# An adaLN block with an S4 convolution and a Mish MLP: the convolution regrouped with 512 channels in the free dimension, constant weights, and corner turns through DRAM

## The chip, the cores and the metric

The program runs on one core of one Trainium2 chip. The metric is the device time of one execution in microseconds (us), as the median of several runs. One execution was also taken with the hardware profiler; all rows of a trace come from that one. Engines are named as in the profile: PE is TensorE's matmul, PEld its weight load, DVE is VectorE, ACT is ScalarE, POOL is GpSimd, and SP is the engine that issues most of the DMA transfers.

## What is computed

The input x has 2048 rows (tokens) of 512 channels, in float32. A vector c gives six vectors of 512 by `silu(c) @ w_mod`: shift, scale and gate for the two halves of the block.

```
sa, ca, ga, sb, cb, gb = split(silu(c) @ w_mod, 6)
h = layernorm(x) * (1 + ca) + sa
x = x + ga * s4(h)              # convolution along the 2048 tokens
h = layernorm(x) * (1 + cb) + sb
x = x + gb * (mish(h @ w1 + b1) @ w2)       # 512 -> 1792 -> 512

s4(u): for each channel d: dt = exp(log_dt), A, B, C of 128 complex states n
  K[d, l] = Re sum_n C[n] * exp(dt A[n] l) * (discretised B)[n],  l = 0 .. 2047
  y[:, d] = causal convolution of u[:, d] with K[d, :], plus u * Dskip
```

The convolution is done as a transform along the tokens, a complex product for each channel, and the inverse transform, with two steps of matmuls each way.

## The kernel before

One function, `s4_block`, holds the whole program; a scheduler orders the instructions of each engine by the priorities that the code sets. It has three stretches.

**The start (0 to about 42 us).** Loads of the parameters (`raw`, L173), of x (`xr`, L195, four transfers of 1 MB) and of weights; the states' parameters are worked out on VectorE (`params`).

**The convolution (to 418 us).** The 512 channels are worked in 32 groups `k` of 16 channels. A slot of the loop holds, for different groups at once:

- Kernel generation. `s_ang` (L344) makes the angles of the powers of exp(dt A) in PSUM as `pang`, two matmuls of 256 columns for each half; `s_ri` (L355, L357) rounds them to whole turns on VectorE, for some groups with ScalarE's help (L349, adding a magic constant), and `s_neg` (L362) subtracts the rounded turns by a matmul with `negid`. `s_sin` (L145, L367) makes sines and cosines into the tile `ec`. `s_mag` multiplies coarse exponentials `co` into the two magnitudes m1 and m2 (L377, L380), and `s_comb` (L387 to L391) multiplies them into `ec`. `s_kgen` (L402) contracts `ec` over the states into `pkg`, ScalarE copies that to `ks` (L407), and `s_ka` (L418) makes the first step of the kernel's transform, `pka`, copied to the tile `gk` (L426).
- The transforms of the input. `s_ua` (L526), a transpose `put` (L536), and the second step with the constant `mf` as the moving or the stationary operand (L546, `pub` and `pkb`). Here the data or `gk` and the constant meet in matmuls of 128 columns, with channels on the partitions.
- The complex product on VectorE (L583 to L585, tile `q`), a transpose `pt` (L590) to `yt`, the first inverse step `pib` (L601), the copy `z` (L603), a transpose `pt` (L611) to `zt`, and the last inverse step `pia` (L637), which is added to x on VectorE (L639). The sum goes to the DRAM tensor `x2d` in another row order.

```
def s_ri(k):
    ri = gen.tile([P, 2, 512], F16, tag="ri", name=f"ri{k}", bufs=1)
    RI[k] = ri
    if RID[k]:
        V.tensor_scalar(ri, PA[k], MAGIC, MAGIC, op0=OP.add, op1=OP.subtract)
...
def s_neg(k):
    for e in range(2):
        T.matmul(PA[k][:, e, :], negid, RI[k][:, e, :], start=False, stop=True, skip_group_check=True)
```

**The MLP (437.86 us to the end).** `ln_load` reads rows from x2d (L774), VectorE takes the statistics and normalises (L781, L790), TensorE transposes (`pln`, L799), and `hf`, `hh` are the modulated rows and their high and low parts. w1 and w2 are kept as high and low parts too (`w1h`, `w1l`, `w2h`, `w2l`), so each product is three matmuls (`pm`, L897, and `po`, L915; 1344 matmuls in all). Mish runs on ScalarE (`mh`), `mah` and `mal` are its two parts, and `ot` is the output, stored by SP (`out`).

Of the kernel before, what the change touches and what calls it, by code (L numbers as in the profile page):

```python
# [28 lines left out]
NCO = 28  # L29
NPRE = 8  # L30
SL = {"p2": 0, "p3": 2, "ls0": 5, "raw": 2, "p0": 5, "ls1": 8, "co0": 6, "vis": 6, "h0": -5, "h1": -2}
HA = 4
NUG = 2
MS = [[3, 0], [5, 2], [0, 4], [1, 6], [2, 8], [4, 9]]
BN = [0, 0, 0, 1]
NS = 1
HS0 = [2, 3, 3, 2]
SPA = 0
RID = [1, 0, 0, 0, 1, 0, 0, 0, 1, 0, 0, 0, 1, 0, 0, 1, 1, 0, 0, 0, 1, 1, 0, 1, 1, 0, 1, 0, 1, 1, 0, 1]
PRI = {"mm": 0.933, "ug": 0.775, "tm": 0.608, "inva": 0.817, "sin": 1.075, "ml": 0.533, "st": 0.933, "par": 0.625, "ri": -0.108, "kgen": 0.05, "p": -0.475, "sr": 1.575, "t2": 0.15, "ls": 0.275, "ut": 0.675}  # L40
PRI0 = {"comb": 0.675, "mc": 0.133, "sm": -0.167, "ua": 0.008, "par": 0.675, "ut": 0.583, "mm": 0.383, "inva": 1.717, "ka": 1.258, "ang": 0.067, "neg": 0.533, "ri": -0.067, "mag": 0.467}
SA = 1
HP = 1
KP = 7
LATE = 2
LAG = 2
UD = [4, 4, 3, 3, 2, 3, 3, 3, 3, 3, 3, 3, 3, 3, 3, 4, 4, 4, 4, 4, 4, 4, 4, 4, 4, 4, 4, 4, 4, 4, 4, 4]
ORDER = [
    ("kgen", 1), ("ks", 1), ("ubu", 3), ("ang", -2), ("ua", -1), ("hs", 0), ("ri", -2), ("misc", 0),
    ("t2", 13), ("mag", -1), ("t1", 9), ("ka", 1), ("par", 0), ("tm", 1), ("neg", -2), ("ut", 2),  # L50
    ("comb", 0), ("ubk", 8), ("inva", 13), ("ug", 4), ("xp", 10), ("sin", -2), ("invb", 9), ("prod", 8),
]


def _constants():
    r = np.arange(32)
    s = np.arange(64)
    j = np.arange(64)
    i = np.arange(32)
    th = 2 * np.pi * ((j[None, :, None] * (4 * r[:, None, None] + 1 + 128 * s[None, None, :])) % 8192) / 8192.0  # L60
    mf = np.zeros((32, 2, 64, 2, 64))
    mf[:, 0, :, 0, :] = np.cos(th)
    mf[:, 1, :, 0, :] = np.sin(th)
    mf[:, 0, :, 1, :] = -np.sin(th)
    mf[:, 1, :, 1, :] = np.cos(th)
    mf = mf.reshape(32, P, P)
    psi = 2 * np.pi * ((i[:, None] * (4 * r[None, :] + 1)) % 128) / 128.0
    da = np.stack([np.cos(psi), -np.sin(psi)], axis=1)
    bdk = np.zeros((4, 32, 2, 4, 32))
    di = np.zeros((2, 2, 4, 16, 32, 4))  # L70
    for t in range(4):
        bdk[t, :, :, t, :] = da
        for hf in range(2):
            for c in range(2):
                di[hf, c, t, :, :, t] = da[:, c, 16 * hf:16 * hf + 16].T / 2048.0
    bdu = bdk.transpose(1, 0, 2, 3, 4)
    ac = np.zeros((4, 32, 32, 32))
    mc = np.zeros((4, 32, 32, NCO))
    fac = np.concatenate([64 * 8 * np.arange(4), 64 * np.arange(8), 8 * np.arange(8), np.arange(8)])
    for d in range(32):  # L80
        ac[0:2, d, d, :] = np.arange(32)
        ac[2:4, d, d, :] = 1
        mc[0:2, d, d, :] = fac
        mc[2:4, d, d, :4] = 1
    z = np.exp(-2j * np.pi * (4 * np.arange(2048) + 1) / 8192)
    one = ((1 + 1j) / (1 - z)).reshape(64, 8, 4)
    one = np.stack([one.real, one.imag]).transpose(2, 0, 3, 1).reshape(4, 2, 512)
    su = np.zeros((4, 32, 2, 512))
    hl = np.zeros((P, 2))
    for e in range(3):  # L90
        m, x = np.frexp(one)
        part = np.ldexp(np.round(m * 256) / 256, x)
        one = one - part
        for n in range(3):
            su[:, 3 * n + e] = part
            hl[3 * n + e::32, :n] = -1
    f = np.float32
    return {
        "su": su.reshape(P, 1024).astype(f),
        "hl": hl.astype(f),  # L100
        "mf": np.ascontiguousarray(mf.transpose(1, 0, 2).reshape(P, 32 * P)).astype(f),
        "mi": np.ascontiguousarray(mf.transpose(2, 0, 1).reshape(P, 32 * P)).astype(f),
        "bdk": bdk.reshape(P, 256).astype(f),
        "bdu": np.ascontiguousarray(bdu).reshape(P, 256).astype(f),
        "di": np.ascontiguousarray(di.transpose(1, 2, 3, 0, 4, 5)).reshape(P, 256).astype(f),
        "ac": ac.reshape(P, 1024).astype(f),
        "mc": mc.reshape(P, 32 * NCO).astype(f),
        "sel": np.tile(np.concatenate([np.eye(32, P, 32 * k) for k in range(4)], axis=1), (4, 1)).astype(f),
        "ident": np.eye(P, dtype=f),
    }  # L110


def _channels():

    d = np.arange(NB * P).reshape(NB, P)
    return np.stack([d[b].reshape(8, 2, 8).transpose(1, 0, 2) if b % 2 == 0 else
                     d[b].reshape(2, 8, 8).transpose(0, 2, 1) for b in range(NB)])
# [3 lines left out]
def s4_block(ctx, tc, io, out):  # L121
# [3 lines left out]
    psum = ctx.enter_context(tc.tile_pool(name="psum", bufs=6, space=bass.MemoryType.PSUM))  # L125
    dram = ctx.enter_context(tc.tile_pool(name="dram", bufs=1, space=bass.MemoryType.DRAM))
    keep = ctx.enter_context(tc.tile_pool(name="keep", bufs=1, side="right"))
    big = ctx.enter_context(tc.tile_pool(name="big", bufs=1))
    left = ctx.enter_context(ExitStack())
    cst = left.enter_context(tc.tile_pool(name="cst", bufs=1))  # L130
    cv = left.enter_context(tc.tile_pool(name="cv", bufs=2))
    right = ExitStack()
    gen = right.enter_context(tc.tile_pool(name="gen", bufs=2, side="right"))

# [15 lines left out]
    x2d = [dram.tile([P, 16, P], F32, name=f"x2d{b}") for b in range(NB)]  # L150
# [6 lines left out]


    ldt = cst.tile([P, NB], F32, name="ldt")
    nc.sync.dma_start(ldt, io["ldt"])  # L160

    def sl8(name):
        return big.tile([P, 2048], F32, tag="sl8", name=name, bufs=2)

    raw = {}

    def load_params(b):
        if b == 0:
            t = gen.tile([P, 16, P], F32, tag="ec", name="raw0", bufs=3)
        else:  # L170
            t = sl8(f"raw{b}").rearrange("p (k n) -> p k n", n=P)
        raw[b] = t
        nc.sync.dma_start(t[:, 0:6, :], io["par"][b].rearrange("p (k n) -> p k n", k=6))  # L173

    load_params(0)
    ident = keep.tile([P, P], F32, name="ident")
    nc.sync.dma_start(ident, io["ident"])
    cT = cst.tile([P, KB], F32, name="cT")
    nc.sync.dma_start(cT, view(io["c"], 0, [[1, P], [P, KB]]))
    dtap = cst.tile([P, 8 * NB, 4], F32, name="dtap")  # L180
    nc.gpsimd.memset(dtap, 0.0)
    nc.sync.dma_start(dtap[0:P:32], io["dtap"].rearrange("t (k m) -> t k m", m=4))
    ac = gen.tile([P, 1024], F32R, name="ac", bufs=1)
    mc = gen.tile([P, 32 * NCO], F32R, name="mc", bufs=1)
    sel = cv.tile([P, 4, P], F32R, tag="yt", name="sel", bufs=1)
    nc.gpsimd.dma_start(sel, io["sel"].rearrange("p (k m) -> p k m", k=4))
    nc.gpsimd.dma_start(mc, io["mc"])
    nc.gpsimd.dma_start(ac, io["ac"])

    def w_mod(col, n, k):  # L190
        return view(io["w_mod"], k * P * 6 * D + col, [[6 * D, P], [1, n]])

    def x_rows(dst, j0, n, b=None):
        w = D if b is None else P
        nc.sync.dma_start(dst, view(io["A_u"], j0 * D + (0 if b is None else b * P),  # L195
                                    [[16 * D, P], [D, n], [1, w]]))

    bdk = cst.tile([P, 256], F32, name="bdk")
    bdu = cst.tile([P, 256], F32, name="bdu")
    di = cst.tile([P, 256], F32, name="di")  # L200
    mf = cst.tile([P, 32, P], F32, name="mf")
    mi = cst.tile([P, 32, P], F32, name="mi")

    def const_col(v, name):
        t = cst.tile([P, 1], F32, name=name)
# [4 lines left out]
    negid = gen.tile([P, P], F16, name="negid", bufs=1)  # L210
    magic = const_col(MAGIC, "magic")


    dt = cst.tile([P, NB], F32, name="dt")
    e_n = cst.tile([P, NB], F32, name="e_n")
    e_r = cst.tile([P, NB], F32, name="e_r")
    e_i = cst.tile([P, NB], I32, name="e_i")
# [14 lines left out]
    S12, S3, PKR = {}, {}, {}  # L232
    
    def params(b, stage):
# [9 lines left out]
        def split(i, j):  # L244
            hi = PKR[b][:, 2 * i:2 * j:2, :]
            (A.copy if b and SPA else V.tensor_copy)(hi, r[:, 10 + i:10 + j, :])
            V.tensor_sub(PKR[b][:, 2 * i + 1:2 * j:2, :], r[:, 10 + i:10 + j, :], hi)
# [13 lines left out]
        if stage == 2:  # L261
            PKR[b] = gen.tile([P, 12, P], F32R, tag="pk", name=f"pk{b}", bufs=1)
# [32 lines left out]
    def load_s(b, half):  # L295
        pk = PKR[b]
        for g in (half, 2 + half):
            d = slice(32 * g, 32 * g + 32)
            if half == 0 or b == 0:
                for i in (g, g + 1) if b else (g,):  # L300
                    S3[b, i] = gen.tile([P, P], F32R, tag="s3", name=f"s3_{b}_{i}", bufs=4)
            S12[b, g] = gen.tile([P, 2, P], F32R, tag="s12", name=f"s12_{b}_{g}", bufs=4)
            if b == 0:
                p = bank("psel")
                for k in range(4):
# [696 lines left out]
```

## Time and profile before

| what | value |
|---|---|
| median of 3 runs | 763.18 us (762.19 to 763.78) |
| the profiled execution | 760.01 us |
| its span | 758.2 us |
| granted TensorE clock, mean | 0.976 |
| transferred | 52.70 MB, mean 70 GB/s |

The span is the time from the first to the last instruction that the profile holds; the 1.8 us between it and the execution's time lie outside. A row of a group gives the line, the engine, the operation, output and input by the program's names, how often it occurs, then the busy time in us and the mean duration in ns, then the idle time ahead of it and what ended that. A row of a timeline gives the start and the duration in us first. A row of a table by stretches gives for each engine the busy time and the number of instructions, then the granted clock, the mean busy share of the 16 DMA engines, and what they moved. A row of a transfer gives its size and the median time from issue to landing.

### The profile page before, as it was taken

Reading aid. Unit: us, or ns where it says so; the run is one execution under the profiler, and the core shown is the slowest. Engines: PE = TensorE matmul, PEld = TensorE weight load, DVE = VectorE, ACT = ScalarE, POOL = GpSimd, SP = SyncE. Lnnn points to the kernel's source line nnn. Section 1 sums busy time; section 2 is a strip of 40 time slices with the busy share of each in tenths; the row PEclk is TensorE's granted clock in tenths of the full one; section 3 lists DMA queues with packets and bytes.
Section 4 is the critical chain, followed back from the end, with each engine's and each line's share of the span. In section 5 each row is a group of like instructions: output and inputs, shape, how many; then the busy total and the mean of one; then the engine's idle time right before and its main releaser. Section 6 shows DMA issues by size and latency. Waiting matters only on the chain.

```text
span 758.2 us, 14266 instructions
## 1 busy us (share of the span) xinstructions
PE 707.0 (93%) x5888; PEld 587.0 (77%) x5888; DVE 450.6 (59%) x918; ACT 428.3 (56%) x689; POOL 52.4 (7%) x108
## 2 busy tenths in 40 slices
PE   0794999999999999999998789999999999999997
PEld 0562879987888898889888568888888888888885
DVE  6889798799899969984464487119211521143113
ACT  3767798989999998776664254233222322232221
POOL 1006203310060200000000000000000000000000
PEclk9987899999999999999999899999999999999999
DMA  9653224200241101110460362002200220002001
GB/s 312 237 194 77 63 66 116 48 8 10 58 112 57 43 2 43 57 57 2 148 215 28 97 187 65 0 1 92 75 1 1 81 87 1 0 1 84 0 1 55
DMA packets 47096, 52.70 MB, mean 70 GB/s; under 512 B 7221, under 2 KB 32825, under 8 KB 46265
## 3 DMA queue, kind: packets, MB, share of 16 engines
q1 hardware_dynamic: 40312, 47.93, 19.6%
q0 software_dynamic: 6720, 3.87, 2.7%
q8 instruction: 46, 0.75, 0.4%
q14 instruction: 18, 0.14, 0.1%
HBM read 41.30 MB, written 8.39 MB: 66 GB/s over the span
## 4 chain that ended last, share of the span: by engine, by line
PE 84%; DVE 7%; ACT 5%; DMA 2%; issue 1%; POOL 0%; SPq 0%; DVEq 0%; ACTq 0%; POOLq 0%
PE pm L897 20%; PE po L915 20%; PE pkb L546 8%; PE pka L418 4%; PE pub L546 4%; PE pua L526 4%; PE pib L601 4%; PE pkg L402 4%; PE pia L637 3%; PE put L536 2%; PE pang L344 2%; PE pang L362 2%; PE pmodp L448 2%; PE pt L611 2%; PE pt L590 2%; ACT ec L145 1%
## 5 line engine op out<-in xcount | busy, mean ns | idle before, releaser
L145 ACT ACTIVATE mh<-pm,b 128x512 f32<-128x512 f32 x56 | 38.6, 690 | 200.0 <-PE pm L897 200.0
L904 DVE TENSOR_TENSOR mal<-mh,mah 128x512 fp32r<-128x512 f32 x56 | 38.7, 691 | 177.6 <-ACT mah L903 177.3
L897 PE MATMUL pm<-hh,w1h 128*128 128x512 f32 x448 | 139.1, 393 | 2.8 <-ACT hh L803 2.8
L897 PEld LDWEIGHTS pm<-hh,w1h 128*128 128x128 f32 x448 | 84.5, 189 | 21.6 <-ACT hh L803 3.5
L915 PE MATMUL po<-w2h,mah 128*128 128x512 f32 x224 | 87.9, 392 | 0.0
L897 PE MATMUL pm<-hh,w1l 128*128 128x512 f32 x224 | 87.5, 392 | 0.0
L915 PE MATMUL po<-w2l,mah 128*128 128x512 f32 x224 | 87.5, 391 | 0.0
L915 PE MATMUL po<-w2h,mal 128*128 128x512 f32 x224 | 87.5, 390 | 0.0
L583 DVE TENSOR_TENSOR q<-pkb,ug 128x512 f32<-128x512 f32 x64 | 41.2, 685 | 47.4 <-PE pkb L546 47.3
L546 PE MATMUL pkb<-mf,gk 128*128 128x128 f32 x256 | 63.3, 389 | 0.2
L546 PEld LDWEIGHTS pkb<-mf,gk 128*128 128x128 f32 x256 | 60.6, 318 | 1.8 <-ACT gk L426 0.5
L603 ACT COPY z<-pib 128x512 f32<-128x512 f32 x32 | 35.1, 1098 | 33.7 <-PE pib L601 33.7
L897 PEld LDWEIGHTS pm<-hh,w1l 128*128 128x128 f32 x224 | 42.5, 190 | 8.8
L915 PEld LDWEIGHTS po<-w2h,mal 128*128 128x128 f32 x224 | 42.1, 188 | 8.6
L915 PEld LDWEIGHTS po<-w2h,mah 128*128 128x128 f32 x224 | 42.1, 188 | 8.4
L915 PEld LDWEIGHTS po<-w2l,mah 128*128 128x128 f32 x224 | 42.1, 188 | 8.2
L387 DVE TENSOR_TENSOR ec<-ec,m 128x1024 f32<-128x1024 f32 x32 | 38.9, 1216 | 9.8 <-ACT ec L145 9.8
L402 PE MATMUL pkg<-ec 128*32 128x64 f32 x2048 | 40.8, 228 | 0.5 <-DVE ec L388 0.3
L526 PE MATMUL pua<-bdu,h 128*128 128x128 f32 x256 | 37.5, 286 | 3.2 <-ACT h L512 3.2
L402 PEld LDWEIGHTS pkg<-ec 128*32 128x32 f32 x2048 | 34.4, 112 | 7.3 <-issue 2.2
L418 PE MATMUL pka<-bdk,ks 128*64 128x128 f32 x512 | 39.5, 289 | 0.1
L377 DVE TENSOR_TENSOR m<-co 128x1024 f32<-128x1024 f32 x32 | 38.9, 1216 | 0.1
(167 smaller groups left out, 1322.5 us busy)
## 6 DMA issues: line engine op xcount, KB each, us to landing
wm<-in_w_mod SPq DMA_DIRECT2D x24, 256.0 KB, 3.1
xr<-in_A_u SPq DMA_DIRECT2D x4, 1024.0 KB, 12.9
out<-ot SPq DMA_DIRECT2D x16, 256.0 KB, 2.0
xp<-in_A_u SPq DMA_DIRECT2D x15, 256.0 KB, 3.0
x2d<-xp SPq DMA_DIRECT2D x15, 256.0 KB, 2.4
xt<-x2d SPq DMA_DIRECT2D x15, 256.0 KB, 4.5
w1s<-in_B_w SPq DMA_DIRECT2D x8, 448.0 KB, 4.0
w2s<-in_B_w SPq DMA_DIRECT2D x14, 256.0 KB, 2.9
```

The lines of the kernel that those rows point to most:

```text
L145: chain(A.activation(out, in_, f, **kw))
L377: V.tensor_mul(m2.rearrange("p d (a b) -> p d a b", a=8), co[:, :, 12:20, None].to_broadcast([P, 16, 8, 8]), co[:, :, None, 20:28].to_broa ...
L387: V.tensor_mul(ec[:, :, :, 32:64], ec[:, :, :, 95:63:-1], m2[:, None, :, 0:32].to_broadcast([P, 2, 16, 32]))
L402: T.matmul(o, ec[:, z, e, 0:32], ec[:, z, e, 32:96], start=(z == 0), stop=(z == 1))
L418: T.matmul(p[64 * cc:64 * cc + 64, o:o + 128], KS[k][:, 64 * m:64 * m + 64], bdk[:, 128 * cc:128 * cc + 128], start=True, stop=True)
L526: T.matmul(p[:, 128 * jj:128 * jj + 128], HS[b][:, 4 * j4 + jj, :], bdu.rearrange("p (a r) -> p a r", r=32)[:, :, 16 * rp:16 * rp + 16], s ...
L546: T.matmul(pv[:, :, r, :], lh(r), mf[:, 4 * s + r, :].rearrange("p (c s) -> p c s", c=2), start=not started, stop=True, skip_group_check=s ...
L583: V.tensor_mul(q, kv[:, c, :, None, :].to_broadcast([P, 4, 2, 64]), ug)
L603: A.copy(Z[b, hf][:, :, :, o:o + 4].rearrange("p j a r -> p r a j"), p.rearrange("p (r a j) -> p r a j", r=4, a=8))
L897: T.matmul(p, w1[wi][:, k, fs], hh[:, hi, k, :], start=(n == 0), stop=(n == 3 * KB - 1))
L904: V.tensor_sub(a[1], h, a[0])
L915: T.matmul(PO[tt][q], a[ai][:, P * q:P * q + P], w2[wi][:, f, :], start=(f == 0 and n == 0), stop=(f == FB - 1 and n == 2))
```

## The change

The convolution is written anew and the loop over slots is split into three stages.

*Kernel generation.* 32 groups as before. The angles come from eight matmuls of 512 columns with 96 rows (`s_ang`, L295): rows of ones times +MAGIC and -MAGIC in the accumulation do the rounding, so `s_ri` and `s_neg` go. One coarse exponential per group has all 32 low magnitudes, so m1 goes. Four small transfers per group put the parameters of 16 channels on the partitions (`load_s`, L270), and 32 more per block of eight groups serve the coarse exponentials (`load_s3`, L277). Beside this the normalised input is transformed: `u_a` on its eight loads of x with the constant `da` stationary and 512 channels moving, written to the DRAM tensor `ud`; `u_b` reads it back in another order, transforms with `mf` stationary, and writes to `fd`. The constants are now the stationary operands everywhere, with 64 columns or 64 rows of TensorE used at a time, and put and both pt are gone.

*Product and inverse.* For each of 16 `q`: `fl` is read from `fd`, `pkb` is the kernel's second step, VectorE makes the complex product in four operations, `pz` is the first inverse step, `z` its copy, which goes to the DRAM tensor `zd`. The second half of the modulation (twelve loads of w_mod) and the loads of w1 stand in between.

*The last inverse step.* `inv_a` reads x and `zl`, makes `pia`, adds, and writes `xd`; the MLP's rows come from `xd`. All loads of x and the output's stores take their rows by `rows()`. The MLP's matmuls are the same; PSUM has 8 banks for it, `mh` has 2 buffers and each of the two parts of `ma` 4.

```diff
+    def rows(src, j0, n, step=1):
+        return view(src, j0 * D, [[16 * D, 4], [64 * D, 32], [step * D, n], [1, D]])
...
+    def load_s(k):
+        b, c = divmod(k, 8)
+        for part in range(4):
+            nc.sync.dma_start(S12[k % 4][16 * part:16 * part + 16].bitcast(F32),
+                              PKR[b][16 * c:16 * c + 16, part, 0:2, :].bitcast(F32))
...
-        for e in range(2):
-            for q in range(2):
-                g, o = 2 * q + c // 4, 8 * (c % 4)
-                T.matmul(p[:, e, 256 * q:256 * q + 256], S12[b, g][:, e, :],
-                         ac[:, 32 * o:32 * o + 256], start=(q == 0), stop=False, skip_group_check=True)
+        for n in range(4):
+            for e in range(2):
+                T.matmul(p[:, e, :], s[:, e, :], ac[:, n, :], start=(n == 0), stop=(n == 3))
...
-        V.tensor_scalar(ri.rearrange("p e (d x) -> p e d x", d=16), EC[k][:, :, :, 32:64], MAGIC, None,
-                        op0=OP.subtract)
...
+    def u_load(n):
+        XT[n] = io4.tile([P, 2, D], F32, tag="i", name=f"x{n}")
+        nc.sync.dma_start(split4(XT[n]), rows(io["A_u"], 2 * n, 2))
...
+    def transform(p, q, rhs):
+        for c in range(2):
+            for r in range(2):
+                T.matmul(p[64 * r:64 * r + 64, c, :], mf[0][:, 2 * q + r, 64 * c:64 * c + 64], rhs(r),
+                         start=True, stop=True)
...
+    def inverse(q):
+        p = pair("pz", f"pz{q}")
+        for c in range(2):
+            for r in range(2):
+                T.matmul(p[:, r, :], mi[64 * r:64 * r + 64, q, c, :], Y[q][64 * r:64 * r + 64, c, :],
+                         start=(c == 0), stop=(c == 1))
...
+    def inv_a(tt):
+        z = zp.tile([P, 2, 4, D], F32, tag="z", name=f"zl{tt}")
+        x = LNX[tt] = mp.tile([P, 4, D], F32, tag="xt", name=f"x{tt}", bufs=3)
+        nc.sync.dma_start(split4(x), rows(io["A_u"], 4 * tt, 4))
...
+        for j in range(4):
+            p = bank("pia")
+            for tl in range(2):
+                T.matmul(p[64 * tl:64 * tl + 64, :], di, z[:, tl, j, :], start=True, stop=True)
+            V.tensor_add(x[:, j], x[:, j], p)
+        nc.sync.dma_start(xd[tt], x)
...
+        nc.sync.dma_start(rows(out, 4 * tt + q, 1), o)
```

`split4` returns its argument.

**Order on SP at the start.** Before: the parameters of two blocks, x in four transfers, small constants; the small loads of the angles' parameters are POOL's.

```order
L173 DMA raw_145<-in_par 128x768
L645 DMA hl<-in_hl 128x2
L195 DMA xr_148<-in_A_u 128x2048
L195 DMA xr_150<-in_A_u 128x2048
L195 DMA xr_152<-in_A_u 128x2048
L195 DMA xr_154<-in_A_u 128x2048
L671 DMA bdk<-in_bdk 128x256
```

After, `wm` being the first half of w_mod and `s_0` to `s_2` the angles' parameters:

```order
L170 DMA wm_108<-in_w_mod 128x2x1536
L157 DMA dtap<-in_dtap 4x128
L170 DMA wm_110<-in_w_mod 128x2x1536
L389 DMA x_143<-in_A_u 128x1x1024
L389 DMA x_145<-in_A_u 128x1x1024
L389 DMA x_147<-in_A_u 128x1x1024
L389 DMA x_149<-in_A_u 128x1x1024
L143 DMA raw_159<-in_par 128x768
L270 DMA s_0_90<-pk_189 16x256 x4
L270 DMA s_1_91<-pk_189 16x256 x4
L270 DMA s_2_92<-pk_189 16x256 x4
L277 DMA s_0_0_210<-pk_189 16x128 x4
```

The twelve and the 32 small loads (seven more rows like the last) moved from POOL's queue to SP's, behind both wm and four loads of x.

**Order on PE in the convolution.** Before, a slot mixes all stages:

```order
L362 MATMUL pang<-ri_1827,negid 128x512
L536 MATMUL put<-ident,u_0_1_868 128x128 x4
L546 MATMUL pkb<-mf,gk 128x2x64 x4
L601 MATMUL pib<-mi,yt_1838 128x128 x4
L402 MATMUL pkg<-ec_1557 32x64 x32
```

After, the same engine in kernel generation, between two of the input's transforms:

```order
L328 MATMUL pkg_1657<-ec_1441 32x64 x15
L340 MATMUL pka_1697<-bdk,ks_1690 64x32x4 x8
L328 MATMUL pkg_1726<-ec_1534 32x64 x17
L295 MATMUL pang_1713<-ac,s_3_93 128x512 x8
L328 MATMUL pkg_1726<-ec_1534 32x64 x15
L340 MATMUL pka_1766<-bdk,ks_1759 64x32x4 x8
```

pkb, pib and pia of the convolution left the slot; they follow when all 32 groups are done.

**Order on SP ahead of the MLP.** Before, row blocks of 256 KB go to `x2d` and come back:

```order
L640 DMA x2d_78<-xt_4791 128x512
L640 DMA x2d_78<-xp_4796 128x512
L929 DMA xr<-x2d_78 128x128 x2
L640 DMA x2d_78<-xp_4796 128x512
L774 DMA xt_5290<-x2d_78 128x512
L640 DMA x2d_78<-xp_4796 128x512
```

After, in transfers of 1 MB (`x_3865` and the two of `zl_3864` stand just ahead):

```order
L608 DMA zl_3917<-zd 64x2x2048 x2
L615 DMA xd<-x_3865 128x2048
L606 DMA x_3918<-in_A_u 128x1x2048
L606 DMA x_3940<-in_A_u 128x1x2048
L608 DMA zl_3939<-zd 64x2x2048
L615 DMA xd<-x_3918 128x2048
L608 DMA zl_3939<-zd 64x2x2048
L606 DMA x_3962<-in_A_u 128x1x2048
L608 DMA zl_3961<-zd 64x2x2048
L615 DMA xd<-x_3940 128x2048
L608 DMA zl_3961<-zd 64x2x2048
L619 DMA xt_4274<-xd 128x2048
```

The whole input x is read once more here, and `xt_4274`, the second block of rows of the MLP, is read back from `xd`. VectorE has its statistics ahead of the first `hf`:

```order
L614 TENSOR_TENSOR x_3940<-x_3940,pia 128x512 x4
L614 TENSOR_TENSOR x_3962<-x_3962,pia 128x512
L627 BN_STATS bst_4347<-xt_4274 128x6
L627 BN_STATS bst_4350<-xt_4274 128x6
L614 TENSOR_TENSOR x_3962<-x_3962,pia 128x512
L628 BN_AGGR mv_3858<-bst_4347 128x2
L628 BN_AGGR mv_3858<-bst_4350 128x2
L614 TENSOR_TENSOR x_3962<-x_3962,pia 128x512
L627 BN_STATS bst_4353<-xt_4274 128x6
L614 TENSOR_TENSOR x_3962<-x_3962,pia 128x512
L642 TENSOR_SCALAR hf<-pln,modt 128x512 x2
```

So `hf`, which in before waits for its own block's transpose alone, now stands behind rows of the next block.

927 lines of the change are left out of this document (340 added, 587 removed).

## Prediction

> **What bounds the kernel now.** I read the page's busy line and its chain first, then a table of busy time by stretches of the span, then TensorE's timeline inside one channel slot, then the groups of VectorE and ScalarE, and last the transfers.
>
> ```profile
> PE 707.0 (93%) x5888; PEld 587.0 (77%) x5888; DVE 450.6 (59%) x918; ACT 428.3 (56%) x689; POOL 52.4 (7%) x108
> PE 84%; DVE 7%; ACT 5%; DMA 2%; issue 1%; POOL 0%; SPq 0%; DVEq 0%; ACTq 0%; POOLq 0%
> core 0: us, PE busy (x) PEld busy (x) DVE busy (x) ACT busy (x) POOL busy (x), PEclk, DMA share, GB/s
> 0.00:20.00 20.00, 0.58 (x3) 0.40 (x3) 13.68 (x72) 6.27 (x8) 2.81 (x12) 1.00 0.91 318
> 0.00:42.00 42.00, 18.08 (x90) 13.02 (x90) 33.30 (x119) 23.72 (x44) 2.81 (x12) 1.00 0.82 285
> 84.00:355.00 271.00, 268.49 (x3544) 232.16 (x3545) 228.98 (x390) 239.62 (x387) 37.43 (x72) 0.99 0.19 52
> 355.00:418.00 63.00, 60.20 (x449) 52.14 (x448) 30.57 (x53) 37.97 (x58) 0.00 (x0) 1.00 0.37 118
> 418.00:438.00 20.00, 14.70 (x57) 9.52 (x58) 10.93 (x45) 4.33 (x7) 0.00 (x0) 0.83 0.33 102
> 438.00:758.20 320.20, 314.32 (x1400) 257.71 (x1400) 108.14 (x230) 92.19 (x142) 0.00 (x0) 0.99 0.14 43
> ```
>
> TensorE is the bound almost everywhere: 268.49 of 271 us in the convolution, 314.32 of 320.2 in the MLP. Only the start, where transfers fill 0.91 of the DMA engines at 318 GB/s, and the 20 us before the MLP wait for anything else. After the start the transfers are light (52 GB/s, then 43). One slot of the convolution, one of 32 channel groups, reads like this on TensorE:
>
> ```profile
> 308.11 1.88 PE L637 MATMUL pia<-zt,di 128*128 128x512 f32 x4
> 309.83 1.05 PE L601 MATMUL pib<-mi,yt 128*128 128x128 f32 x8
> 310.82 1.17 PE L402 MATMUL pkg<-ec 128*32 128x64 f32 x64
> 311.92 0.39 PE L553 MATMUL pub<-su,sab 32*128 32x512 bf16 x1
> ...
> 313.15 0.72 PE L344 MATMUL pang<-ac,s 128*128 128x256 f32 x4
> 313.70 0.38 PE L526 MATMUL pua<-bdu,h 128*128 128x128 f32 x2
> ...
> 315.56 1.09 PE L418 MATMUL pka<-bdk,ks 128*64 128x128 f32 x16
> 316.59 0.60 PE L362 MATMUL pang<-ri,negid 128*128 128x512 f16 x2
> ```
>
> From one start to the next: a 512-column f32 record 0.43 us (1.72 for 4; a matmul is two records), pkg 1.10, pka 1.03, a 256-column angle matmul 0.14 (0.55 for 4).
>
> **What is removed.** The rounding of the angles on VectorE and ScalarE, the product m1, the negid matmuls, and the transposes put, pt and pt:
>
> ```profile
> L380 DVE TENSOR_TENSOR m<-co 128x512 f32<-128x512 f32 x32 | 21.8, 682 | 0.4 <-ACT co L145 0.4
> L355 DVE TENSOR_SCALAR ri<-pang 128x1024 f16<-128x1024 f32 x14 | 17.0, 1216 | 0.8 <-PE pang L344 0.7
> L357 DVE TENSOR_SCALAR ri<-ec 128x1024 f16<-128x1024 f32 x18 | 12.4, 691 | 4.5 <-ACT ec L349 4.5
> L349 ACT ACTIVATE ec<-pang,magic 128x1024 f32<-128x1024 f32 x18 | 20.1, 1118 | 3.4 <-PE pang L344 3.3
> ```
>
> That is 51 us of VectorE and 20 of ScalarE, all beside a full TensorE, so alone it is worth nothing. The gain must come from TensorE, and the convolution is regrouped so thoroughly that I cost the new stages, not differences.
>
> **The start.** SP now issues, ahead of the 12 + 32 small loads that the first angles and the first eight coarse exponentials need, 6.0 MB: two 1.57 MB loads of w_mod, two of par (0.39), four of A_u (0.52). POOL's queue adds 1.0.
>
> ```profile
> 2.12 0.43 SPq L179 DMA_DIRECT2D cT<-in_c  x1
> 2.60 0.66 SPq L182 DMA_DIRECT2D dtap<-in_dtap  x1
> SPq L671 <- DMA cT<-in_c: 2.7, 1, 2.7
> s<-pk POOLq DMA_DIRECT2D x48, 16.0 KB, 2.3
> 35.01 1.23 DVE L387 TENSOR_TENSOR ec<-ec,m 128x1024 f32<-128x1024 f32 x1 [2.38 <-ACT ec L145]
> 36.16 1.22 DVE L391 TENSOR_TENSOR ec<-ec,m 128x1024 f32<-128x1024 f32 x1
> 37.29 0.69 DVE L357 TENSOR_SCALAR ri<-ec 128x1024 f16<-128x1024 f32 x1
> 37.89 0.68 DVE L380 TENSOR_TENSOR m<-co 128x512 f32<-128x512 f32 x1
> L145 ACT ACTIVATE co<-pco 128x448 f32<-128x448 f32 x32 | 14.9, 560 | 1.2 <-PE pco L325 1.1
> L148 ACT ACT_TABLE_LOAD x7 | 9.0, 1283 | 0.1
> L145 ACT ACTIVATE ec<-pang 128x1024 f32<-128x1024 f32 x32 | 33.4, 1043 | 0.0
> ```
>
> The first row pair gives SP's pitch, 0.45 to 0.48 us a transfer. The third says that bdk, the 12th transfer, waited for cT, the 4th: a transfer waits until the one eight places ahead has landed. So the seventh small load waits for the last A_u load. 7.0 MB at 318 GB/s are 22 us, with the first issue 24. Then 36 small loads x 0.45 = 16, 2.3 to land, the last coarse exponential 560 x 768/448 = 0.96, a table 1.28 and two sines 2.2: the first product on VectorE stands at about 47 to 48 us (35.01 before).
>
> **The price that no row shows.** All A_u loads and all output stores now go through rows(): four outer runs on the DRAM side against 128 on the SBUF side. Every large transfer of before has 128 on both. If the work is still shared by 16 engines, 1 MB takes 3.3 us (318 GB/s). If it is cut in four, it takes 12: 318/0.91/16 = 21.8 GB/s for each engine, times 4. The one transfer of before with four outer runs is dtap, and it is the one that SP needed longer to issue (0.66 against 0.43). It is the nearest row, so I take 12 us and keep 3.3 for the range. A small transfer that is spread over all engines queues behind the A_u loads on those four too. The Trainium skill, page "DMA: Bandwidth & Descriptors", section "Why a DMA increments its semaphore by 16 and not by 1", says that a transfer uses the largest number up to 16 that divides the slowest dimension of both sides, which is four here; by it the sum below ends at 803, without it at 747, and no run here shows it yet. In the start the four engines then carry 4.9 MB/16 + 2.1 MB/4 = 0.83 MB, which takes 38 us instead of 22: first product at 63.
>
> **Generation of the kernels.** VectorE per channel group: three operations of 1024 elements at a pitch of 1.13 (37.29 - 36.16) and two of 512 at 0.60, together 4.6; x 32 = 147. Layer norm of eight A_u loads (about 4.1 each by the same pitches) 33, parameters of the later blocks 12: 192 us. TensorE: 8 angle matmuls of 512 columns 2.2 + 1.10 + 1.03 = 4.3, below 4.6. But over groups 20 to 30 the forward transforms of all 16 q are added, 1.45 per group, 1.75 us each if the two 64-column halves overlap as pka's do (16 records in 1.03): 6.8 against 4.6, so 11 x 2.2 = 24. At each of three visits eight exponentials and two tables (10 us of ScalarE) cost VectorE some 5: 15. Together 231.
>
> **Products and inverse.** VectorE 2 x 1.13 + 2 x 0.60 = 3.5 per q, TensorE the same, transfers 1.05 MB. After the last gk there move 6.3 MB of fl (a few are ahead), 8.4 of zd, 3.1 of w_mod, 3.7 of w1: 21.5 MB, 68 us at 318 GB/s. pz of the second q stands behind 12 w_mod loads that share two buffers, and both first w1l subtractions stand ahead of q = 3 on VectorE: some 11 lost. The last q's product, inverse and store add 6. Together 85.
>
> **The way to the MLP.** Here everything turns through DRAM on one queue: x (4 MB), zl (8), xd (3) and xt_4274 (1) pass before the first hf, because VectorE has the statistics of xt_4274 ahead of it and TensorE all four pia ahead of pln.
>
> ```profile
> 426.57 0.69 DVE L639 TENSOR_TENSOR xt<-xt,pia 128x512 f32<-128x512 f32 x1 [10.20 <-PE pia L637]
> 437.86 1.22 PE L897 MATMUL pm<-hh,w1h 128*128 128x512 f32 x4 [2.10 <-ACT hh L803]
> out<-ot SPq DMA_DIRECT2D x16, 256.0 KB, 2.0
> x2d<-xp SPq DMA_DIRECT2D x15, 256.0 KB, 2.4
> xr<-in_A_u SPq DMA_DIRECT2D x4, 1024.0 KB, 12.9
> ```
>
> In before it is 11.3 us from the first add to the first pm. Now 16.8 MB at 318 GB/s are 53, plus 2.4 to land and 3 to hf, hh: 58. With A_u on four engines these carry 4.2/4 + 12.6/16 = 1.84 MB, 84 us; with the landing, the tail and 3 us of waits in the chain 92.
>
> **MLP.** The same 1344 matmuls at the same rate: 320 from its window, 3 for fewer buffers (mh and ma have 2 and 4). With four engines the last four stores of 256 KB queue up at 3.0 us each: 7 more.
>
> **The sum.** Four engines: 63 + 231 + 85 + 92 + 330 = 801, with the 1.8 us outside the span (760.01 - 758.2) 803, against 760.01. Sixteen: 48 + 231 + 85 + 58 + 323 = 745, so 747. The median of the runs, 763.18, lies 3.2 above the profiled one: 806, or 750. The convolution does lose its TensorE bound, and what it saves there (438 us to the first pm before) goes into DRAM round trips during which TensorE stands.
>
> **Rivals.**
> - *A, the forecast (0.55)*: 806. For it: four outer runs in each of 12 loads and 16 stores. Against: no large transfer of that form in the trace.
> - *B, sixteen engines anyhow (0.25)*: 750, the other side. The place is the A_u loads at the start and before the MLP. Between 3.3 and 12 us for 1 MB the sum rises by 56, 6.4 per us, so it decides from 5.3 us on: below that the kernel is faster.
> - *C, sixteen engines, but the halves do not overlap or the 16-partition loads cost 0.66 (0.10)*: the inverse at 3.5 instead of 1.75 per q and the forward transforms likewise give 16 x 1.75 = 28 at most; 36 small loads at 0.21 more and the same at three visits give some 20. About 775, slower. For: dtap's 0.66, and no row of 64 input rows. Against: pka's overlap.
> - *D, VectorE alone is the bound and the transfers are quick (0.10)*: the 24 + 15 and 11 fall away and the two chains overlap better, 750 - 45 = 705.
>
> Under 0.2%, 1.5 us, this measurement can't tell a change from none. Faster: all of D, 0.17 of B, 0.03 of the rest, 0.30. Same 0.03. Slower 0.67. The range goes from B's lower half, 735, to A with part of C, 832, and leaves out D and some of either end; A's own range is 785 to 832.
>
> **What would show it.** Right: A_u loads of 1 MB landing after some 12 us and of 0.5 MB after 6 or more, a first L307/L313/L317 product near 63 us, an idle TensorE of some 90 us ahead of the first pm1, stores of 3 us or more. Generation should show VectorE busy at about 190 of 231 us. Wrong: 1 MB landing in 4 us, first product under 50; or a first pm1 before 440, whatever the loads do. An MLP stretch over 340 would say that I missed a wait there.

## The result, and the profile after

The changed kernel takes 956.51 us (median of 4, 950.63 to 957.99) against 762.68 us before (median of 4). The ratio is 1.254, with a 95% interval of 1.248 to 1.261. Slower was forecast, by 43 us; it is slower by 194, and the time lies far above the range. The profiled execution took 950.63, with a span of 948.5. Of the runs below, the second ones of experiments 2 and 4 (950.19 and 899.99) fell into a slower state that a kernel shows in some executions, so only the first ones of those two are compared.

The busy line and the chain of the page after:

```profile
PE 680.1 (72%) x4912; PEld 444.3 (47%) x4912; DVE 426.4 (45%) x814; ACT 311.5 (33%) x417; POOL 20.5 (2%) x44
PE 54%; DMA 20%; SPq 10%; DVE 6%; ACT 5%; issue 3%; POOL 1%; POOLq 0%; ACTq 0%; DVEq 0%
```

TensorE was busy for 93% of the span and is for 72%, which is still 680 us against 707: little was saved, though all transposes of the convolution are gone, and its idle time grew from 51 to 268 us. VectorE went from 451 to 426 us. In the chain stand now 20% of DMA and 10% of SP's own queue, which were 2% and nothing.

The stretches after, in the columns of the table in the prediction (start, generation, products, the way to the MLP in two pieces, MLP):

```profile
0.00:64.00 64.00, 16.14 (x46) 7.02 (x46) 31.28 (x158) 14.17 (x19) 2.81 (x12) 0.68 0.40 117
64.00:375.00 311.00, 241.69 (x3116) 149.27 (x3118) 202.22 (x337) 181.32 (x231) 17.73 (x32) 0.82 0.40 117
375.00:475.00 100.00, 81.59 (x280) 23.04 (x278) 65.57 (x72) 23.03 (x25) 0.00 (x0) 0.95 0.75 231
475.00:600.00 125.00, 17.42 (x48) 5.24 (x48) 15.09 (x37) 0.56 (x1) 0.00 (x0) 0.58 0.66 130
600.00:625.00 25.00, 15.99 (x70) 10.28 (x70) 14.98 (x32) 7.51 (x13) 0.00 (x0) 0.79 0.53 191
625.00:948.00 323.00, 307.30 (x1355) 249.47 (x1354) 97.26 (x179) 84.86 (x130) 0.00 (x0) 0.98 0.12 37
```

Two things stand out. In the generation no engine is full: TensorE 242 of 311 us at a granted clock of 0.82, VectorE 202. And from 475 to 600 us almost nothing computes, while the DMA engines are busy two thirds of the time and move only 130 GB/s. Against the terms of the sum:

| stage | forecast | measured | read in the trace at |
|---|---|---|---|
| first product on VectorE | 63 | 69.7 | start of L313 |
| generation | 231 | 305.1 | to the end of the last gk copy, 374.8 |
| products, to the last zd landed | 85 | 104.6 | 479.4 |
| to the first pm | 92 | 136.4 | 615.8 |
| MLP | 330 | 332.7 | 948.5 |

The miss is 147.5 us: 7 + 74 + 20 + 44 + 3. The experiments go after the large ones.

### The profile page after: what moved, and what is told of

Its sections match the earlier page's. It is cut to its first block, busy times and chain, and to the rows that moved or that the text cites. A ratio compares the mean times of both kernels' runs of the same rounds, so it can differ in the third digit from the quotient of the medians.

```text
span 948.5 us, 12350 instructions
## 1 busy us (share of the span) xinstructions
PE 680.1 (72%) x4912; PEld 444.3 (47%) x4912; DVE 426.4 (45%) x814; ACT 311.5 (33%) x417; POOL 20.5 (2%) x44
## 4 chain that ended last, share of the span: by engine, by line
PE 54%; DMA 20%; SPq 10%; DVE 6%; ACT 5%; issue 3%; POOL 1%; POOLq 0%; ACTq 0%; DVEq 0%
PE pm L655 16%; PE po L672 16%; DMA zl<-zd 9%; SPq L277 7%; PE pang L295 7%; DMA x<-in_A_u 3%; PE pub L429 3%; PE pkg L328 3%; DMA raw<-in_par 2%; PE pka L340 2%; PE pua L407 2%; SPq L389 2%; PE pia L613 1%; PE pkb L429 1%; ACT ec L109 1%
## 5 line engine op out<-in xcount | busy, mean ns | idle before, releaser
L613 PE MATMUL pia<-zl,di 128*64 128x512 f32 x64 | 22.4, 865 | 115.9 <-DMA zl<-zd 115.9
L295 PE MATMUL pang<-ac,s 96*128 96x512 f32 x256 | 80.5, 463 | 27.9 <-DMA s<-pk 22.1
L655 PEld LDWEIGHTS pm<-hh,w1h 128*128 128x128 f32 x448 | 84.0, 188 | 22.7 <-DVE hh L644 2.7
L295 PEld LDWEIGHTS pang<-ac,s 96*128 96x128 f32 x256 | 53.8, 222 | 52.7 <-issue 33.6
L313 DVE TENSOR_TENSOR ec<-ec,m 128x1024 f32<-128x1024 f32 x32 | 39.1, 1221 | 73.5 <-ACT ec L109 73.5
L613 PEld LDWEIGHTS pia<-zl,di 128*64 128x64 f32 x64 | 6.8, 200 | 131.9 <-issue 131.6
L340 PE MATMUL pka<-bdk,ks 128*64 128x128 f32 x512 | 40.7, 304 | 33.3 <-POOL ks L333 33.2
L643 ACT ACTIVATE hh<-pln,modt 128x512 fp32r<-128x512 f32 x16 | 12.4, 780 | 149.1 <-DMA w2s<-in_B_w 139.4
L614 DVE TENSOR_TENSOR x<-x,pia 128x512 f32<-128x512 f32 x16 | 10.7, 682 | 111.0 <-PE pia L613 92.6
L328 PEld LDWEIGHTS pkg<-ec 128*32 128x32 f32 x2048 | 40.5, 119 | 27.2 <-issue 20.9
L340 PEld LDWEIGHTS pka<-bdk,ks 128*64 128x64 f32 x512 | 31.8, 150 | 43.4 <-POOL ks L333 42.1
L429 PE MATMUL pub<-ur,mf 128*64 128x512 f32 x128 | 38.3, 665 | 17.9 <-DMA ur<-ud 17.9
L328 PE MATMUL pkg<-ec 128*32 128x64 f32 x2048 | 49.9, 239 | 1.5 <-DVE ec L314 1.1
```

The lines of the kernel that those rows point to most:

```text
L295: T.matmul(p[:, e, :], s[:, e, :], ac[:, n, :], start=(n == 0), stop=(n == 3))
L313: V.tensor_mul(ec[:, :, :, 32:64], ec[:, :, :, 95:63:-1], m[:, None, :, 0:32].to_broadcast([P, 2, 16, 32]))
L328: T.matmul(o, ec[:, z, e, 0:32], ec[:, z, e, 32:96], start=(z == 0), stop=(z == 1))
L340: T.matmul(p[64 * cc:64 * cc + 64, :, 4 * m:4 * m + 4], KS[k][:, 64 * m:64 * m + 64], bdk[:, cc, :], start=True, stop=True)
L429: T.matmul(p[64 * r:64 * r + 64, c, :], mf[0][:, 2 * q + r, 64 * c:64 * c + 64], rhs(r), start=True, stop=True)
L613: T.matmul(p[64 * tl:64 * tl + 64, :], di, z[:, tl, j, :], start=True, stop=True)
```

## Experiments

All times are in us. Each kernel was run twice, one of these with a profile; the changed kernel stands at 951 to 958. The two times of a kernel lie up to 7 us apart, so smaller differences between times are not read. A span is that of the profiled run.

### 1. A_u and the output in four pieces each

```diff
+    def four(src, j0, n, tile_, store=False):
+        for a in range(4):
+            v = view(src, j0 * D + 16 * D * a, [[64 * D, 32], [D, n], [1, D]])
+            t = tile_[32 * a:32 * a + 32]
...
+                nc.sync.dma_start(t, v)
...
-        nc.sync.dma_start(split4(x), rows(io["A_u"], 4 * tt, 4))
+        four(io["A_u"], 4 * tt, 4, x)
```

The same for `u_load` and the stores.

> Every load of A_u and every output store is issued as four transfers of 32 partitions each, so that the outermost count is 32 on both sides; the bytes and their places are the same. Theory 'four engines': in the profile of the changed kernel the DMA share stands at 0.25 for some 50 us ahead of the MLP (514 to 530, 546 to 557, 566 to 575, 582 to 586, 594 to 606) and 1 MB of A_u moves at 105 GB/s; in four pieces these loads use all engines, the way from the last zd to the first pm falls from 136 us to about 90, the first product comes 10 us earlier, the last store lands 5 us earlier: about 890 us in place of 951 to 957. Rival 'DRAM side': the strides of these loads are what is slow, not their number of engines; then the time stays within 10 us of 951, and is a little longer by the 72 additional issues of 0.6 us.

Measured: 896.17 and 900.12, span 898.0, 50 less than 948.5. The way from the last z copy to the first pm fell from 140 to 93 us, the first product came at 57.4 instead of 69.7, and the end came 4.5 us sooner after the last pm. The generation itself became 14 us longer; the additional issues may do that, but in experiments 6 and 13, which have them too, it is only 4 to 5 longer, so the cause is open. Two stretches of the changed kernel ahead of the MLP, and behind them two of this one:

```profile
490.00:510.00 20.00, 0.00 (x0) 0.00 (x0) 0.00 (x0) 0.00 (x0) 0.00 (x0) 0.50 1.04 127
515.00:530.00 15.00, 6.53 (x16) 1.95 (x16) 4.25 (x8) 0.00 (x0) 0.00 (x0) 0.55 0.25 56
```

```profile
485.00:500.00 15.00, 0.00 (x0) 0.00 (x0) 0.17 (x1) 0.00 (x0) 0.00 (x0) 0.50 1.02 216
520.00:525.00 5.00, 0.00 (x0) 0.00 (x0) 0.00 (x0) 0.00 (x0) 0.00 (x0) 0.50 1.01 297
```

The 0.25 in the second row is four of sixteen engines, at work alone: those that had A_u to move before their share of zl. In four pieces this stretch is gone, and while A_u moves (last row) all engines are busy and carry 297 GB/s. Four engines are shown. By the rule of the Trainium skill that the prediction cites ("DMA: Bandwidth & Descriptors", section "Why a DMA increments its semaphore by 16 and not by 1") it had to be four, and the trace agrees, with its 0.25.

SP's queue at the start shows the four engines too, in the changed kernel and then in four pieces (start, duration, line, transfers in a row):

```profile
5.15 14.80 SPq L389 DMA_DIRECT2D x<-in_A_u  x4
20.00 4.76 SPq L143 DMA_DIRECT2D raw<-in_par  x1
24.88 18.11 SPq L270 DMA_DIRECT2D s<-pk  x12
43.04 20.17 SPq L277 DMA_DIRECT2D s<-pk  x32
```

```profile
5.14 16.99 SPq L140 DMA_DIRECT2D x<-in_A_u  x16
22.37 0.35 SPq L152 DMA_DIRECT2D raw<-in_par  x1
23.00 7.60 SPq L279 DMA_DIRECT2D s<-pk  x12
30.65 20.17 SPq L286 DMA_DIRECT2D s<-pk  x32
```

The twelve loads took 18.11 us to issue behind the four-engine loads and take 7.60 now. The 32 of them take 20.17 us in both: 0.63 each, and not the 0.45 that the prediction used.

In the MLP the stores were late as well. Waits of VectorE for a free output tile, changed kernel and four pieces (total, times, longest):

```profile
DVE ot L680 <- DMA out<-ot: 26.9, 8, 5.5
```

```profile
DVE ot L689 <- DMA out<-ot: 3.0, 2, 1.7
```

They fell by 24 us, and yet from the first to the last pm it takes 308.3 and 308.7: TensorE didn't wait for these.

### 2. The small loads on POOL's queue

```diff
-            nc.sync.dma_start(S12[k % 4][16 * part:16 * part + 16].bitcast(F32),
+            nc.gpsimd.dma_start(S12[k % 4][16 * part:16 * part + 16].bitcast(F32),
```

and the same in `load_s3`.

> The 256 small loads of 16 partitions (load_s, load_s3) are issued by POOL in place of SP. Theory 'SP is the bound at the block changes': each burst of 28 to 32 such loads holds SP for 17.6 to 20 us at 0.62 us each, and the gaps between products at groups 8, 16 and 24 are 24, 23 and 43 us where a group takes 5.3; off SP they fall to some 10 us each, the start gains 10 to 15: kernel generation from 305 to about 250 us, the whole about 885. Rival 'the visits themselves': the eight exponentials, two tables and the matmuls ahead of them make these gaps; then the time falls by less than 15 us. POOL's own add into ks may be late behind its issues, which would take some of the gain back.

Measured: 933.46, span 931.7, 17 less: far from the 885 of the first theory, and a little over the 15 that the rival allowed. A block is eight groups, and at its change (a visit) the coarse exponentials of the next eight are made. The gaps between products, from one start of L313 to the next, at the three block changes were 21.5, then 21.7 and 16.5 around group 16, then 19.2 and 19.3 around group 24, in sum no less than before. The 17 us are spread: the first product came 5 us earlier, and the generation, the products and the way to the MLP were 7, 3 and 2 us shorter. The queue of POOL at the first block change, in this run:

```profile
108.69 13.59 POOL L277 DMA_DIRECT2D s<-pk  x28 [1.66 <-DMA s<-pk]
```

The burst only moved, with 0.49 us a transfer, and POOL's add into ks stands behind it. This does not tell the theories apart; experiment 5 takes most of the issues away.

### 3. zd with padded rows

```diff
-    zd = dram.tile([2, 32, 64, D], F32, name="zd")
+    zd = dram.tile([2, 32, 68, D], F32, name="zd")
```

with 68 for 64 in its views.

> zd has 68 rows in place of 64 per block, so that the 64 partitions of a zl load are 136 KB apart in DRAM, not 128 KB; 6% more DRAM is laid out, the same bytes move. Theory 'stride': with all 16 engines busy the zl loads move 126 to 150 GB/s (8 KB in 0.9 to 1.1 us, against 0.31 us where x or xd move alone) because the rows stand a power of two apart; padded they take 0.31 to 0.4 us each and the way to the MLP falls by some 25 us: about 927. Rival 'half the partitions': the load is slow since it writes 64 partitions at a time; then 8 KB still take 0.9 us or more and the time stays within 5 us of 951.

Measured: 953.87 and 955.80. No change, and the same stretch looks the same:

```profile
490.00:510.00 20.00, 0.00 (x0) 0.00 (x0) 0.00 (x0) 0.00 (x0) 0.00 (x0) 0.50 1.03 128
```

127 GB/s before, 128 padded. The stride theory falls.

### 4. These three together

> All three edits together: four pieces, the small loads on POOL, zd padded. If all three theories hold and add up: 951 - 60 - 70 - 27, about 795 us, slower than before's 763 still. If the stride or the four engines don't hold: 820 to 850.

Measured: 874.88, span 873.1: above 820 to 850, as the second edit alone gave 17 us and the third nothing.

### 5. Few small loads

```diff
+    def dump(b):
+        nc.sync.dma_start(pkd[b], PKR[b].bitcast(F32))
...
-        for part in range(4):
-            nc.sync.dma_start(S12[k % 4][16 * part:16 * part + 16].bitcast(F32),
-                              PKR[b][16 * c:16 * c + 16, part, 0:2, :].bitcast(F32))
+        nc.sync.dma_start(S12[k % 4][0:64].rearrange("p e n -> p (e n)").bitcast(F32),
+                          view(pkd[b], 16 * c * 12 * P, [[3 * P, 4], [12 * P, 16], [1, 2 * P]]))
```

`load_s3` reads its block with four transfers.

> The split parameters of each block go to DRAM in one transfer, and come back in one transfer per group (64 partitions) and four per block, so that SP issues 52 small transfers in place of 256; everything else as in the changed kernel. With POOL as the issuer (the run before) a burst still took 13.6 us on its queue and POOL's add into ks stood behind it, so that run did not take the bursts away. Theory 'number of issues': the gaps at groups 8, 16 and 24 fall from 24, 23 and 43 us to 10 to 13, generation from 305 to 255 or less, the first product comes 10 to 20 us earlier; in all about 885 us. Rival 'the visits themselves' (exponentials, tables, the clock): the gaps stay above 18 us and the time above 930.

Measured: 917.71 and 922.89, span 915.4, 33 less. Generation took 278.6 instead of 305.1, and the gaps at the block changes are 19.9, 22.7 and 22.7 us (24.3, 22.6 and 42.8 before): between the two theories. The third gap was made by SP. In the changed kernel, VectorE and SP there, and TensorE's wait in the same stretch:

```profile
270.89 1.22 DVE L313 TENSOR_TENSOR ec<-ec,m 128x1024 f32<-128x1024 f32 x1 [1.47 <-ACT ec L109]
304.29 1.23 DVE L307 TENSOR_TENSOR m<-co 128x1024 f32<-128x1024 f32 x1 [29.84 <-ACT co L109]
313.67 1.23 DVE L313 TENSOR_TENSOR ec<-ec,m 128x1024 f32<-128x1024 f32 x1 [8.15 <-ACT ec L109]
```

```profile
267.60 19.21 SPq L277 DMA_DIRECT2D s<-pk  x28
...
290.06 1.81 SPq L419 DMA_DIRECT2D ur<-ud  x3
```

```profile
PE pub L429 <- DMA ur<-ud: 17.9, 1, 17.9
```

The reads of ud stood behind the burst of 28, TensorE's transform pub waited 17.9 us for them, and the matmuls of the coarse exponentials, the exponentials and VectorE stood behind pub. What is left at each block change, some 20 us, is its own: between the two table switches of ScalarE, 115.17 and 132.13 in this run, lie eight exponentials, most of which wait for their matmuls, and no sine runs.

### 6. zl on two queues, beside the four pieces

```diff
-            nc.sync.dma_start(z[64 * th:64 * th + 64],
+            (nc.gpsimd if th else nc.sync).dma_start(z[64 * th:64 * th + 64],
```

> The four-piece loads, and beside it the second half (64 partitions) of each zl load is issued by POOL, so that both halves of the partitions are written at once. With the loads in four pieces alone, zl filled all 16 engines at 206 to 220 GB/s, 0.62 us for 8 KB, where x and xd took 0.31. Theory 'half the partitions': both halves in flight bring 300 GB/s or more, and the way to the MLP falls from 93 to about 80 us: 885 in place of 898. Rival 'the DRAM side or the form of the read': 8 KB stay at 0.6 us and more, and the time at 898 within 5.

Measured: 880.20 and 880.34 against 896 to 900; the way from the last z copy to the first pm 85 us instead of 93. Of the 19.5 us between the spans, 9 lie in the generation and 3 in the products, which the edit does not touch; why is open. The 9 are not due to zl on two halves, as experiment 13 shows them too; the 8 us on the way to the MLP are what the edit is read by. While zl moves:

```profile
488.00:500.00 12.00, 5.42 (x16) 1.67 (x16) 3.30 (x6) 0.00 (x0) 0.00 (x0) 0.58 1.02 284
```

284 GB/s against 216 with one half at a time (experiment 1). Experiment 13 asks whether it was the halves or the queues.

### 7. Pieces, two queues, few small loads

> All that is found so far together: four pieces, zl on two queues, few small loads. If the three effects add up: 898 - 13 - 60, about 825 us; if the small loads don't matter, 885.

Measured: 843.80 and 846.92, span 841.5. The gains of the single edits in the spans, 50, 33 and 20, would give 845: they add up. The 825 was too low because it took the small loads at 60.

### 8. No exponentials at the block changes

```diff
-        tables("natural_log_exp_and_others")
+        if b == 0 or b + 1 < NB:
+            tables("natural_log_exp_and_others")
...
         for c in range(8):
-            coarse(8 * b + c)
+            if b == 0:
+                coarse(c)
+            else:
+                CO[8 * b + c] = CO[c]
...
-            at(k0 + 5, load_s3, b + 1)
```

> The coarse exponentials of the blocks 1 to 3 are left out, with their 96 small loads, their matmuls and the last table switch; the groups 8 to 31 use the values of block 0 (so the convolution kernels of three quarters of the channels are other numbers). It measures what a block change costs in all. In the changed kernel the products at groups 8, 16 and 24 come 24, 23 and 43 us after the ones before, where a group takes 5.3 to 8; with 52 small transfers in place of 256 they still took 20, 23 and 23. Theory 'block changes': without them these gaps are 6 to 10 us, generation falls from 305 to about 240 us, and the time from 951 to about 885. Rival 'late transforms': the third gap is the forward transform waiting for its reads and returns elsewhere; then generation stays above 265 us.

Measured: 915.02 and 919.23, span 917.1. Generation took 270.5 us instead of 305.1: not 240, and above the 265 that the rival set. Without the breaks no gap is above 13 us, but the mean of all is 8.2 where the undisturbed groups 17 to 21 of the changed kernel take 5.4: norms, transforms and reads that ran in the breaks now run between the groups. So the exponentials with their loads, their matmuls and one of the three switches (two stay, for the parameters) cost 35 us net, not the 74 by which the three gaps exceed a group's time, and not the 15 of the prediction.

### 9. The modulation behind the products

```diff
-    for k in range(KB):
-        mod_row(k)
...
             load_w1(q // 4, q // 2 % 2)
+    pm = pair("pz", "pmod1")[:, 0, :]
+    for k in range(KB):
+        mod_row(k)
```

> The second half of the modulation (twelve loads of w_mod through two buffers, 12 matmuls) stands behind the sixteen products instead of among the first ones. Theory 'pz waits for w_mod': in the changed kernel the first z copy comes 32 us after the last gk, where the later pace is 4.5 us per q; without the twelve loads it comes after about 12 us, the last z copy 16 to 20 us earlier, and the loads now run while zl is on its way: 935 us. Rival 'transfers are the bound': the first q's are slow because the DMA engines are full, or the loads come due again at the end; then the first pm moves by less than 8 us.

Measured: 922.30 and 922.99, span 920.8, 28 less. From the last gk to the last z copy 76.7 us instead of 100.8, so the twelve loads cost 24 there. The first pm came at 569.4, 46 us earlier, as the way from the last z copy is 25 us shorter too. But part of that is only moved: the last load of A_u is now waited for behind the first pm, and 19 us are given back in the MLP (327.2 from the first to the last pm, against 308.3):

```profile
PE pm L654 <- DVE x L613: 15.2, 1, 15.2
```

```profile
DVE x L613 <- DMA x<-in_A_u: 15.5, 1, 15.5
```

VectorE waits for the last load of A_u on its four engines, with the next `hh` behind it, and TensorE waits for that.

### 10. Pieces, two queues, few small loads, modulation last

> The version with four pieces, two queues for zl and few small loads (843.8 to 846.9), and the modulation behind the products as well: 828 if that gain adds up, 845 if the transfers are the bound there.

Measured: 838.35 and 840.39. It gains some 6, near the scatter, and not 17.

### 11 and 12. The add into ks on VectorE

```diff
-        nc.gpsimd.tensor_add(KS[k][:, 0:256:64], KS[k][:, 0:256:64], dtap[:, k])
+        V.tensor_add(KS[k][:, 0:256:64], KS[k][:, 0:256:64], dtap[:, k])
```

> The add of dtap into ks goes back from POOL to VectorE, as in the kernel before. In the changed kernel TensorE's pka waits 33 us in 27 places for that add on POOL. Theory 'the hop to POOL': without it these waits fall and generation is 10 to 20 us shorter, about 935. Rival 'TensorE is not what sets the pace': VectorE and ScalarE set it, pka only waits earlier or elsewhere, or the add now stands behind a long VectorE operation; then the time stays within 6 us of 951 to 957 or grows.

Measured: 961.15 and 961.33, no faster. TensorE's wait for `ks` only changes its name; the changed kernel's row and this one's:

```profile
PE pka L340 <- POOL ks L333: 33.2, 27, 4.0
```

```profile
PE pka L340 <- DVE ks L333: 31.4, 25, 5.5
```

> The version with four pieces, two queues, few small loads and the modulation last (838.4 to 840.4), and the add of dtap on VectorE: 828 if that gain adds up, 840 if it does not. Before stays faster by 70 us or more.

Measured: 815.78 and 815.83, the fastest of all, and 24 us faster than experiment 10, whose generation took 288 us where this one took 262. It remains slower than before (ratio 1.070, 1.066 to 1.074): 95 us still pass from its last z copy to its first pm.

### 13. The same half on two queues

```diff
+            for s, eng in enumerate((nc.sync, nc.gpsimd)):
+                eng.dma_start(z[64 * th + 32 * s:64 * th + 32 * s + 32],
+                              view(zd, (16 * th + 4 * tt + 32 * 64 * s) * D, [[64 * D, 32], [32 * D, 2], [D, 4], [1, D]]))
```

> The four-piece loads (896 to 900 us), and each zl load of 64 partitions cut into two of 32, one issued by SP and one by POOL, first the lower 64 partitions and then the upper. Two queues work at once, as in the run with zl on two queues (880), but here both write the same half of the partitions. Theory 'half the partitions': it stays at 206 to 220 GB/s while zl moves, and the time at 895 to 900. Rival 'one queue is too little for this form of load': it rises to 280 GB/s as there, and the time falls to 880 to 885.

Measured: 891.45 and 896.62; the way to the first pm 93.5 us, as with one queue. (The generation was 10 us shorter than in experiment 1, as in experiment 6.)

```profile
486.00:506.00 20.00, 2.83 (x8) 1.09 (x10) 0.95 (x3) 0.00 (x0) 0.00 (x0) 0.50 1.02 221
```

221 GB/s with two queues in one half, 216 with one queue, 284 with two queues in both halves. It is the halves: while zl fills 64 of the 128 partitions at a time, all engines are busy and move three quarters of what they move into both halves at once.

### 14. Few small loads, and the add on VectorE

> The changed kernel with few small loads (917.7 to 922.9) and the add of dtap on VectorE. That add alone made the changed kernel 5 to 10 us slower, and the version with everything else 24 us faster. Theory 'the bursts hide it': with the bursts of small loads gone, the hop to POOL is on the path of every group, and the time falls to 895 to 905. Rival 'it is the modulation's place or the pieces that matter, or chance of the order': it stays at 915 to 925.

Measured: 912.97 and 920.25, against 917.71 and 922.89 without the add. The difference is within the scatter, so the bursts did not hide it. Why the add is worth 24 us among the other edits and nothing clear here is open.

## Where the prediction was right and wrong

**Right in its kind.** The bound moved as forecast, from TensorE to round trips through DRAM and to SP's queue; the four engines, the late first product, the idle TensorE ahead of the MLP and the unchanged MLP are all in the trace. Rival B (sixteen engines anyhow) falls with the 0.25 of experiment 1, and D with the generation. But even the four pieces, which are what B describes, stand at 896 to 900 and not at 750. In the prediction the four engines alone made the kernel slower; without them it would still be slower by some 135 us, for reasons that were not in the sum. To that extent the right direction was luck.

**The steps that failed.** Two terms are most of the miss. The generation was priced by its busiest engine, with everything else beside it at little or nothing (231; it took 305). The way to the MLP was priced by bytes at one rate for each DMA engine (92; it took 136). What the runs showed in their place follows by stage.

**The start, 63 against 70.** The issue of a small load was priced at 0.45 us and is 0.63 (experiment 1). For the 36 loads of that sum this is 6.5 us, nearly the whole difference.

**The generation, 231 against 305.** Each block change was priced at 5 us on VectorE beyond a group; without the exponentials generation is 35 us shorter, and 26 go with the small loads. These overlap, since without the exponentials 96 of the loads are gone too. The dtap row, 0.66, was in the prediction and served for the four engines, but not for the 16-partition loads that it resembles as much; rival C had this number and gave it a chance of 0.10, in the wrong place: as time of issue, not as a queue in which the reads for TensorE wait.

The group's own pace was mis-sized too. The prediction took VectorE's 4.6 us, as TensorE's 4.3 fit beside it. In the undisturbed groups of the changed kernel the chain that ended last runs in a loop (one turn, without its pieces called issue or ACTq, all under 0.1 us):

```profile
240.54 0.38 ACT ks L332
240.99 0.32 POOL ks L333
241.35 1.09 PE pka L340 x16
242.44 0.79 PE pkg L328 x35
243.23 2.05 PE pang L295 x8
245.28 0.65 PE pkg L328 x28
246.00 0.38 ACT ks L332
```

One turn takes 5.46 us: 4.58 on TensorE, and 0.88 for the hop through ScalarE and POOL, during which TensorE stands in front of pka. The prediction put that hop at nothing. Moved to VectorE (experiment 11) it stays: TensorE waits 31.4 us for `ks` in all, and 33.2 with POOL. Over 32 groups the 0.86 us above 4.6 would be 27 us, an estimate; no run takes the hop away. TensorE's granted clock is not the reason here: it is 1.00 from 232 to 254 us. Elsewhere it is lower, as its mean of 0.82 says (0.99 in the convolution before): from 225 to 230 us it is 0.50, and the eight angle matmuls there take 3.78 us instead of 2.05. What that costs in all was not tried, and how the rest of the 74 us divides is open.

**The way to the MLP, 92 against 136.** The 84 us for the bytes assumed 318/0.91/16 = 21.8 GB/s of every engine. zl goes into 64 partitions at a time, and that is 216 GB/s alone, 13.5 for each engine (experiment 1), and 127 in all beside the loads on four engines. That A_u takes four engines was right, and so was its 12 us for 1 MB, nearly: where A_u moves alone the four carry 93 GB/s, which is 11.3 us for 1 MB.

```profile
570.00:575.00 5.00, 0.00 (x0) 0.00 (x0) 0.00 (x0) 0.00 (x0) 0.00 (x0) 0.50 0.24 93
```

That the other engines' transfers run at their usual rate beside them was wrong. With A_u on all engines (experiment 1) the way takes 90 us where the sum for sixteen engines had 58, and with both halves of zl at once (experiment 6) 82.

**The products, 85 against 105.** The loss to the twelve w_mod loads was put at 11 and is 24 (experiment 9); the other 7 us are open. The two halves of TensorE do overlap, against rival C: the inverse takes 1.85 us per q where the granted clock is 1.00 (16 records in 3.70, two q), near the 1.75 of the prediction:

```profile
406.81 3.70 PE L558 MATMUL pz<-y,mi 64*128 64x512 f32 x16 [0.72 <-ACT mrow L578]
```

**The MLP, 330 against 333.** Of the 7 us that were put on the last stores, four pieces gain 4.5 back behind the last pm.

Two sums of the rivals are off, without bearing on the forecast: C's small loads come to 28 us or more, not some 20, and D's terms to 50, not 45.

## What to carry over

Before a transpose is given up for a trip through DRAM, price the trip by its form and not by its bytes alone: how many outer runs both sides have, how many partitions it fills at a time, and what stands behind its issue on the queue. Price a stage by the longest loop through its engines, not by the busiest of them: here a group took 5.46 us and not 4.6, and TensorE's busy time fell by 27 us while its idle time grew by 217. And where a table switch divides a loop into blocks, look at the whole stretch between the switches, since here no sine ran in it.

## What was not expected of the hardware

- A load of A_u on four engines did not only run slowly itself. Beside it, zl on all engines and A_u together moved 127 GB/s with every engine busy (zl without it 216). Why is open.
- While zl filled 64 partitions at a time it moved 216 to 221 GB/s, with one queue or two; both halves at once gave 284.
- The stride of zd's rows in DRAM, 128 or 136 KB, made no difference (127 and 128 GB/s).
- SP needed 0.63 us to issue a load of 16 partitions, POOL 0.49.
